# A retention attention and its channel mix on one core: blocks 6 to 11 take K once for turned keys and state products

## The chip, the cores and the metric

The kernel runs on one core of one Trainium2 chip. The metric is the device time of one execution in microseconds (us), and lower is better. Five engines of the core work beside one another: PE multiplies matrices, DVE and ACT work on vectors, POOL (GpSimd) does here one product and otherwise issues DMAs, and SP issues DMAs alone. Each engine takes its own instructions in the order in which the program holds them and waits at one until what it needs is there. PE loads one operand of a product as weights (LDWEIGHTS) and then streams the other past it (MATMUL); such a pair is called a pass here. What PE computes lands in PSUM, which has eight banks of 512 float32 per partition; a bank can be written anew once its readers are done.

## The reference

A retention with a recurrent state and per-head decay, and behind it a channel mix with squared ReLU and a gate:

```python
for t in range(S):                              # B, H, S, D = 4, 8, 768, 64
    state = gamma * state + einsum('bhd,bhe->bhde', k[:, :, t], v[:, :, t])
    y[:, :, t] = scale * einsum('bhd,bhde->bhe', q[:, :, t], state)
x = y.transpose(0, 2, 1, 3).reshape(B, S, H * D)
x_prev = concatenate([zeros, x[:, :-1]], axis=1)
xk = mu_k * x + (1 - mu_k) * x_prev             # xr with mu_r
k = maximum(xk @ w_k, 0)                        # 512 -> 1024
v = k * k @ w_v                                 # 1024 -> 512
out = 1 / (1 + exp(-(xr @ w_r))) * v
```

## The kernel before

The 4 x 768 tokens are cut into twelve blocks of 256, three to a batch: blocks 0, 3, 6 and 9 begin a batch. In a block the retention is done by products instead of one token after another. Per block n:

- `lq`, `lk`, `lv` load Q, K and V (float16 for Q and K, cast by GpSimd's DMAs). `vs` multiplies V by the decay and rounds it (L253).
- `Tq` and `Tk` turn Q and K with PE: a product with an identity (L278; L272 in blocks 0 to 3), `Eq` and `Ek` copy the turned halves from PSUM to SBUF (L241, on ACT). A turn of a block is 32 passes that give 64 columns each.
- `S` multiplies turned keys and queries (L318 in blocks 6 to 11), `M` masks the result and takes it to SBUF (L354, DVE).
- `C` is the state product K x V (L366 in blocks 6 to 11, L384 in 2 to 5): K is the stationary operand, V the moving one; 32 passes of 64 columns, 24 where the batch ends. `U` adds the earlier state (L419, DVE, or an ACT copy at L243), `G` applies the block's decay (L424, ACT).
- `I` and `J` multiply the carried state and Q (L441), `Y` the masked scores and V (L462, L478, L489); they add up in one pair of banks. `D` scales that into x, channels on partitions (L514, DVE).
- `dx` and `X` make the shifted mixes xk and xr (L529, L558, L552, DVE). `K.n.g` are the keys of the channel mix (L572 where two blocks are taken together, L582 else), `Qa` their ReLU out of PSUM (L591, ACT), `Qb` the square (L599, L603, ACT). `R` is the gate product (L612) and `s` its sigmoid (L618, ACT), `V.n.t.h` one half of a value product (L624, four passes of 512 columns), `O` the gated result (L630, DVE), `st` its store on SP's queue.
- `z` are products of zeros that fill PE's time near the start (L703, L710).

The order of all this is written out by hand: a string ORDER of some 750 words, which the kernel's last loop goes through from front to back. A word is a piece of the work, the PSUM banks behind an @ and the engine behind a ~ (v DVE, a ACT, p GpSimd's queue, s SP's queue, none PE). `C.4@67` is the state product of block 4 in banks 6 and 7; `Qa.2.0~a` the ReLU of the first keys of block 2 on ACT. So each engine gets its pieces in the string's order, and a piece waits for the pieces it reads from, for the readers of the bank that it writes, and for a DMA's buffer to come free. What a load waits for is what last read its buffer: Q, K and V have four buffers each, the scaled V three, block n using number n mod 4 or n mod 3.

Masks and identities are built on DVE at the start by comparing a row of counts with a column of numbers (`masks`, L680), `mu8` receives the mix factors, which PE turns and ACT copies (L691, L694).

Of the kernel before, what the change touches and what calls it, by code (L numbers as in the profile page):

```python
# [33 lines left out]
lk.3~p vs.2~v Tq.2@1 X.1.1.2~v K.1.3@6 K.1.0@0 C.2@7 U.2.0~v lv.3~p Eq.2~a S.2.1@23 M.2.1~v S.2.0@45
M.2.0~v Qb.0.3~a lv.4~p K.1.1@1 X.1.1.1~v Qa.1.0~a t.0.1.0~a K.1.2@7 I.2@23 Qb.0.1~a Qa.1.1~a wv.0~p
Qb.0.2~a Tq.4@01 Eq.4~a Y.2 Qa.1.3~a Qb.1.1~a X.0.1.3~v X.1.1.3~v R.1.1@4 Tk.4@01 Ek.4~a J.2 R.1.0@6
Qa.1.2~a s.1.0~a X.0.1.2~v X.0.1.1~v X.0.1.0~v R.0.1@5 s.0.1~a s.1.1~a R.0.0@7 s.0.0~a S.4.1@01
Qb.1.0~a D.2~v dx.2~v X.2.0.2~v X.2.0.0~v S.4.0@23 Tq.3@4 Eq.3~a X.2.0.1~v wv.1~p X.2.0.3~v Tk.3@7
lq.5~p Ek.3~a K.2.2@5 Qa.2.2~a K.2.3@4 M.4.1~v M.4.0~v Qa.2.3~a Qb.2.3~a lk.6~p S.3.1@67 M.3.1~v
S.3.0@01 vs.3~p C.3@23 U.3.0~a Qb.2.2~a K.2.1@4 Qa.2.1~a K.2.0@2 Qa.2.0~a I.3@45 lq.6~p vs.4~v  # L40
C.4@67 U.3.1~v X.2.1.1~v V.0.1.0@3 M.3.0~v V.1.0.0@2 G.3~a U.4.0~v I.4@01 X.2.1.3~v U.4.1~v J.3
Qb.1.3~a Y.4 Qb.2.0~a lk.5~p X.2.1.2~v X.2.1.0~v Y.3 D.3~v dx.3~v V.0.0.0@7 V.0.1.1 O.0.1~v Tq.5@45
J.4 D.4~v dx.4~v R.2.0@6 Qb.2.1~a V.0.0.1 O.0.0~v X.3.0.1~v Eq.5~a Qb.1.2~a V.1.0.1 X.3.0.2~v
O.1.0~v Tq.6@01 Eq.6~a Tk.6@45 Ek.6~a st.0.0~s lk.7~p st.1.0~s V.1.1.0@3 V.1.1.1 O.1.1~v s.2.0~a
R.2.1@0 s.2.1~a lv.5~p X.3.0.0~v X.3.0.3~v Tk.7@67 Ek.7~a G.4~a S.6@45 M.6~v Tk.5@23 Ek.5~a vs.5~v
V.2.0.0@0 K.3.2@1 Qa.3.2~a K.3.0@6 S.5.0@23 M.5.0~v S.5.1@45 C.5@1 U.5.0~v K.3.3@7 Qb.3.2~a Qa.3.0~a
lq.7~p K.3.7@6 Qa.3.3~a Qa.3.7~a lv.6~p lq.8~p vs.6~v M.5.1~v V.2.0.1 st.0.1~s I.5@67 O.2.0~v
st.2.0~s C.6@23 U.6.0~a U.6.1~v U.6.2~v K.3.6@1 Qa.3.6~a lk.9~p X.3.1.3~v Y.5 Tq.7@45 Eq.7~a U.6.3~v
X.3.1.2~v I.6@01 J.5 X.3.1.0~v D.5~v X.3.1.1~v Qb.3.3~a G.6~a V.2.1.0@2 K.3.1@3 V.2.1.1 O.2.1~v
Qb.3.7~a Qa.3.1~a Qb.3.1~a dx.5~v K.3.4@4 K.3.5@5 Qa.3.5~a X.5.0.0~v X.5.0.3~v R.3.1@2 s.3.1~a  # L50
lv.7~p Qa.3.4~a X.5.0.1~v Qb.3.4~a R.3.0@5 R.4.0@2 s.3.0~a s.4.0~a Qb.3.0~a X.5.0.2~v vs.7~v K.5.2@4
S.7@67 st.1.1~s M.7~v Qb.3.5~a Y.6 Qb.3.6~a lv.10~p C.7@23 U.7.0~v X.5.1.1~v Qa.5.2~a K.5.0@5
R.4.1@6 Qa.5.0~a D.6~v s.4.1~a V.4.0.0@4 V.4.0.1 V.3.1.0@5 U.7.1~v Qb.5.0~a X.5.1.3~v U.7.2~v I.7@01
X.5.1.2~v U.7.3~v Tq.8@67 Eq.8~a X.5.1.0~v O.4.0~v lv.8~p vs.8~v Qb.5.2~a lq.10~p lk.8~p Tk.8@23
Ek.8~a V.3.1.1 V.3.0.0@4 C.8@67 O.3.1~v st.2.1~s st.3.1~s Y.7 dx.6~v D.7~v Tq.10@23 V.3.0.1 Eq.10~a
G.7~a dx.7~v X.6.0.2~v V.4.1.0@5 R.5.1@2 s.5.1~a K.5.3@0 Qa.5.3~a R.5.0@2 U.8.0~v O.3.0~v V.4.1.1
lv.9~p lk.10~p lq.9~p Tk.10@01 s.5.0~a U.8.1~v X.6.0.1~v Ek.10~a X.6.0.0~v Tk.9@23 Ek.9~a K.5.1@7
# [27 lines left out]
def kernel(  # L85
# [51 lines left out]

    Q16 = ring("q16_", 4, [H, 2 * D], F16)
    K16 = ring("k16_", 4, [H, 2 * D], F16)
    V32 = ring("v32_", 4, [H, 2 * D], F32)  # L140
    VS = ring("vs_", 3, [2, H, D], F16)
# [17 lines left out]
    mu8 = const.tile([P, P], F32, name="mu8")  # L159
# [17 lines left out]
    count = OS(3)[:, 0:P]  # L177

# [223 lines left out]

    def carried(n, c):
        return TG[c if half(n) else 2 * c](n)

    def summed(e, n, c):
        src = banks("C", n)
        if half(n):
            src = src[:, c % 2, c // 2 * NJ * D : (c // 2 + 1) * NJ * D]
            last = c == 3  # L410
        else:
            src = (src[:, c] if more(n) else src)[:, 0 : NJ * D]
            last = c == 1
        src = src.rearrange("p (j d) -> p j d", j=NJ)
        to = T32(n) if last else carried(n, c + 1)
        if c == 0 and first(n):
            copy(e, to, src)
        else:
            nc.vector.tensor_tensor(out=to, in0=src, in1=carried(n, c), op=ALU.add)  # L419
# [81 lines left out]
    def yout(e, n, u=None):  # L501
# [16 lines left out]
        )  # L518

# [154 lines left out]
    def masks(e, part):  # L674
        for out, col, op in (
            ((ident, 0, ALU.is_equal),),
            ((causal[:, 0], 1, ALU.is_ge), (causal[:, 1], 1, ALU.is_gt)),
            ((step, 2, ALU.is_ge), (below, 0, ALU.is_ge)),
        )[part]:
            e.tensor_scalar(  # L680
                out=out, in0=count[:, 0 : out.shape[-1]], scalar1=mark[:, col : col + 1], scalar2=None, op0=op
            )
# [50 lines left out]
    def load_wk(e, h):  # L733
        f = slice(h * dff // 2, (h + 1) * dff // 2)
        nc.gpsimd.dma_start(out=wk16[:, :, f], in_=wks[:, :, f])
# [4 lines left out]
    def load_wv(e, h):  # L740
# [59 lines left out]
```

## Time and profile before

| what | value |
|---|---|
| median of 3 runs | 153.06 us |
| lowest and highest | 152.80 and 153.37 us |
| the profiled execution: time, span | 152.84 us, 151.1 us |
| granted PE clock over the span | 1.000 |
| PE, DVE, ACT, POOL busy | 143.7, 127.7, 103.4, 55.3 us |
| value products (L624) | 184 passes, 44.1 us |
| gate, keys together, keys (L612, L572, L582) | 23.4, 23.0, 23.2 us |
| turns of Q and K in 64 columns (L278) | 256 and 256 passes, 3.6 and 3.4 us |
| state products of blocks 6 to 11 (L366) | 176 passes, 2.7 us |

The span runs from the first to the last instruction of the profiled execution; 1.74 us of its time lie around it. Busy times are unions: passes overlap in the pipeline, so that a pass has a mean of, say, 195 ns and 256 of them 3.6 us all the same. In a timeline a row is a run of like instructions with its start, its length, its engine, its line, the operation with its tiles, the stationary operand's size for PE (64*64), the shape and the count; [0.65 <-DVE tg L419] is idle time ahead of it and what ended it. The length of a run of passes has the pipeline's last end in it, so what a run costs is read from its start to the start of the next.

### The profile page before, as it was taken

To read this page: it belongs to the slowest core of one execution; us is meant where nothing else is said; L and a number is where in the kernel's file an instruction comes from. 1 tells how busy PE (TensorE), PEld (TensorE's weight loads), DVE (VectorE), ACT (ScalarE), POOL (GpSimd) and SP (SyncE) were. 2 spreads that over 40 slices of the span, in tenths; PEclk is the share of its full clock that TensorE was granted. 3 is DMA by queue.
4 is the path that set the end of the run, shared out by engine and by line. 5 is a ranking of instruction groups with operands and counts; after the bars stand their busy time and mean duration, and the time that the engine had idled before them with its cause. 6 is when DMAs were issued, how large, how long until landed. Compare 5 with 4: busy or idle time off the path is not lost.

```text
span 151.1 us, 5533 instructions
## 1 busy us (share of the span) xinstructions
PE 143.7 (95%) x2426; PEld 82.6 (55%) x2426; DVE 127.7 (85%) x211; ACT 103.4 (68%) x195; POOL 55.3 (37%) x65
## 2 busy tenths in 40 slices
PE   7968799999999999999999999999999999999991
PEld 3345487748754554547465564548456444655450
DVE  7976999999999999999999999999799999400432
ACT  3475979799944895879567786999604756839420
POOL 7954988478867209996700000000000000000000
PEclk9999999999999999999999999999999999999999
DMA  4999999999999999999999019311000005500433
GB/s 135 229 235 192 204 233 195 169 250 213 196 166 206 232 267 101 265 299 196 229 172 126 4 40 282 105 38 42 0 4 0 4 0 205 212 0 0 152 130 139
DMA packets 45624, 22.16 MB, mean 147 GB/s; under 512 B 37400, under 2 KB 41248, under 8 KB 45600
## 3 DMA queue, kind: packets, MB, share of 16 engines
q0 software_dynamic: 38704, 14.42, 74.7%
q1 hardware_dynamic: 6592, 7.21, 14.3%
q8 instruction: 19, 0.31, 0.8%
q10 hardware_dynamic: 304, 0.18, 0.4%
q14 instruction: 5, 0.04, 0.1%
HBM read 24.16 MB, written 6.29 MB: 202 GB/s over the span
## 4 chain that ended last, share of the span: by engine, by line
PE 73%; DMA 12%; POOL 11%; issue 2%; DVE 0%; POOLq 0%
PE ps L624 27%; PE ps L572 14%; PE ps L612 12%; PE ps L582 8%; DMA q<-in_q_dram 7%; DMA v<-in_v_dram 5%; PE ps L278 3%; POOL q L235 3%; POOL k L230 2%; PE ps L441 2%; POOL vs L253 2%; PE ps L366 1%; PE ps L462 1%; POOL v L230 1%; PE ps L642 1%
## 5 line engine op out<-in xcount | busy, mean ns | idle before, releaser
L624 PE MATMUL ps<-wv,k2s 128*128 128x512 f16 x184 | 44.1, 380 | 0.0
L591 ACT ACTIVATE kr<-ps 128x512 f32<-128x512 f32 x48 | 27.8, 594 | 12.4 <-PE ps L582 6.4
L624 PEld LDWEIGHTS <-k2s 128*128 128x128 f16 x184 | 17.1, 98 | 18.9 <-ACT k2s L603 0.4
L630 DVE SCALAR_TENSOR_TENSOR os<-ps,rs 128x512 f32<-128x512 f32 x23 | 15.7, 684 | 11.8 <-ACT rs L618 9.5
L612 PE MATMUL ps<-wr,xr 128*128 128x512 f16 x96 | 23.4, 379 | 0.0
L582 PE MATMUL ps<-xk,wk 128*128 128x256 f16 x192 | 23.2, 273 | 0.0
L572 PE MATMUL ps<-xk,wk 128*128 128x512 f16 x96 | 23.0, 379 | 0.0
L618 ACT ACTIVATE rs<-ps 128x512 f32<-128x512 f32 x24 | 13.6, 597 | 12.5 <-PE ps L612 12.4
L230 POOL DMA_DIRECT2D k<-in_k_dram x20 | 17.7, 902 | 11.5 <-PE ps L384 6.9
L582 PEld LDWEIGHTS <-wk 128*128 128x128 f16 x192 | 18.0, 98 | 3.8
L241 ACT COPY qT<-ps 128x1024 f16<-128x1024 f16 (+1 forms) x13 | 12.3, 946 | 9.4 <-PE ps L278 7.8
L558 DVE SCALAR_TENSOR_TENSOR xr<-dx,mu,xT 128x256 f16<-128x256 f32 (+1 forms) x32 | 17.9, 577 | 0.1
L230 POOL DMA_DIRECT2D v<-in_v_dram x18 | 16.1, 912 | 3.5 <-DMA wr<-in_moe_w_r_dram 1.9
L558 DVE SCALAR_TENSOR_TENSOR xk<-dx,mu,xT 128x256 f16<-128x256 f32 (+1 forms) x32 | 17.0, 580 | 0.2
L354 DVE TENSOR_TENSOR a<-ps,c_sb 128x1024 f16<-128x1024 f32 (+1 forms) x14 | 14.5, 1065 | 0.9 <-PE ps L339 0.6
L603 ACT ACTIVATE k2s<-kr 128x512 f16<-128x512 f32 x24 | 14.8, 631 | 0.3
L572 PEld LDWEIGHTS <-wk 128*128 128x128 f16 x96 | 9.1, 98 | 10.6
L612 PEld LDWEIGHTS <-xr 128*128 128x128 f16 x96 | 9.1, 98 | 10.6 <-DVE xr L558 0.3
L599 ACT ACTIVATE k2s<-kr 128x512 f16<-128x512 f32 x24 | 14.5, 626 | 0.3
L241 ACT COPY kT<-ps 128x1024 f16<-128x1024 f16 (+1 forms) x13 | 12.2, 944 | 2.8 <-PE ps L272 1.9
L529 DVE TENSOR_TENSOR dx<-xT 128x1024 f32<-128x1024 f32 x11 | 13.4, 1221 | 0.2
L253 DVE TENSOR_TENSOR vs<-v,csm_sb 128x1024 f16<-128x1024 f32 x10 | 12.2, 1217 | 0.2
(73 smaller groups left out, 165.9 us busy)
## 6 DMA issues: line engine op xcount, KB each, us to landing
out_dram<-os SPq DMA_DIRECT2D x23, 256.0 KB, 2.4
v<-in_v_dram POOLq DMA_DIRECT2D x18, 256.0 KB, 7.6
q<-in_q_dram POOLq DMA_DIRECT2D x11, 256.0 KB, 8.3
k<-in_k_dram POOLq DMA_DIRECT2D x21, 128.0 KB, 8.7
v<-in_v_dram POOLq DMA_DIRECT2D x2, 512.0 KB, 6.9
wk<-in_moe_w_k_dram POOLq DMA_DIRECT2D x2, 512.0 KB, 10.7
wv<-in_moe_w_v_dram POOLq DMA_DIRECT2D x2, 512.0 KB, 9.6
wr<-in_moe_w_r_dram POOLq DMA_DIRECT2D x1, 512.0 KB, 9.5
```

Source lines behind the costliest of these rows:

```text
L230: e.dma_start(out=dst[:, :, i * D : i * D + D], in_=src[:, i * P : i * P + P].rearrange("h p d -> p h d"),)
L241: e.copy(out=out, in_=in_)
L253: e.tensor_tensor(out=VS(n), in0=V32(n).rearrange("p h (i d) -> p i h d", i=2), in1=gks[:, int(half(n) or wide(n)), :, :, None].to_broadca ...
L354: nc.vector.tensor_tensor(out=a_full(n)[:, i, :, j0:j1], in0=pairs(banks("S", n, i, j0))[:, :, j0:j1], in1=(below if wide(n) else causal[: ...
L558: nc.vector.scalar_tensor_tensor(out=XM[w](k)[:, j, t0:t1], in0=DX(k)[:, j, t0:t1], scalar=mu[:, w * NCO + j : w * NCO + j + 1], in1=x[:, ...
L572: nc.tensor.matmul(banks("K", n, g), lhsT=wk16[:, co, g * P : g * P + P], rhs=XM[0](k)[:, co, :], start=(co == 0), stop=(co == NCO - 1),)
L582: nc.tensor.matmul(pz[:, i, :], lhsT=wk16[:, co, fo * P : fo * P + P], rhs=XM[0](k)[:, co, m * TM + t0 : m * TM + t1], start=(i == 0 and c ...
L591: nc.scalar.activation(out=kr, in_=banks("K", n, g, *u), func=AF.Relu)
L603: nc.scalar.activation(out=K2(n)[:, w * g : w * g + w, t0:t1], in_=kr.rearrange("p a t -> p (a t)").rearrange("p (i t) -> p i t", i=w), fu ...
L612: nc.tensor.matmul(banks("R", n, tb), lhsT=XM[1](k)[:, co, t : t + P], rhs=wr16[:, co, :], start=(co == 0), stop=(co == NCO - 1),)
L624: nc.tensor.matmul(banks("V", n, tb), lhsT=K2(n)[:, fo, tb * P : tb * P + P], rhs=wv16[:, fo, :], start=(fo == 0), stop=(fo == NFO - 1),)
L630: nc.vector.scalar_tensor_tensor(out=OS(2 * n + tb), in0=banks("V", n, tb), scalar=1.0 / (KSC * KSC), in1=RS(2 * n + tb), op0=ALU.mult, op ...
```

## The change

**One pass of K for two products (blocks 6 to 11).** `Tk`, `Ek` and `C` go; `TC.n.i` and `Ec.n.i` come, i the half of the block. K is the stationary operand, as in `C`, and the moving one is 128 columns wide: 64 of an identity and 64 of V. So a pass gives the turned K and the state product side by side. Each of the three buffers of scaled V has got 64 columns more in front, which hold an identity (`VI`, place 0), and the moving operand is taken with a step from the identity to the head's V.

```diff
+    def VS(n):
+        return VI(n)[:, 1:].rearrange("p (i h) d -> p i h d", i=2)
-    VS = ring("vs_", 3, [2, H, D], F16)
+    VI = ring("vs_", 3, [2 * H + 1, D], F16)
...
+    def both(n, i):
+        return banks("TC", n, i).rearrange("p u (j x t) -> p u j x t", j=NJ, x=2)
+
+    def turned_state(e, n, i):
+        ps = both(n, i)
+        for j in range(NJ):
+            for u in range(2):
+                for a, h, jo, hp in heads(j):
+                    k = 1 + i * H + h
+                    x = slice(0, 2) if more(n) or not (u and i) else slice(0, 1)
+                    nc.tensor.matmul(
+                        ps[low(a), u, j, x], lhsT=K16(n)[low(u), h, i * D : i * D + D],
+                        rhs=VI(n)[low(u), 0 : k + 1 : k][:, x],
+                        start=(j == 0), stop=(j == NJ - 1), skip_group_check=True,
+                    )
+
+    def turned_k_part(e, n, i):
+        copy(
+            e, KT(n)[:, :, i].rearrange("c j (u p) -> c u j p", u=2), both(n, i)[:, :, :, 0],
+        )
```

Both results lie in a pair of banks per half, four banks to a block; the turned keys are float32 there. `Ec` copies them to SBUF as float16, one copy for each half. `U` reads the states out of the same banks, with a step:

```diff
+        if merged(n):
+            src = both(n, c // 2)[:, c % 2, :, 1]
```

The identities of the three buffers are built in `cm.2` behind the two masks there:

```diff
-            ((step, 2, ALU.is_ge), (below, 0, ALU.is_ge)),
+            ((step, 2, ALU.is_ge), (below, 0, ALU.is_ge))
+            + tuple((VI(i)[:, 0], 2, ALU.is_equal) for i in range(3) if MERGED),
```

**A fence.** `w.n` on ACT reads a few elements of the bank pair of I into a small tile, between `I.n` and `Y.n`:

```diff
+    def fence(e, n):
+        us = slice(0 if half(n) or not first(n) else 1, 2)
+        e.copy(out=fenced[:, us], in_=pairs(banks("I", n))[:, us, :, 0:C:W])
```

`mu8` shares a tile with a result buffer, and `wk` is loaded by words that name quarters; the two transfers are the old ones.

**Order.** The zero products are other ones: before, three long ones ahead of the first turn, then a short one and five pairs of short ones; now two long and two short ones ahead of the first turn, then one long and twelve short ones in groups of 1 to 3. The pair directly ahead of Tq.1 is gone. Apart from these the first 196 pieces stand in the order that they had, but the PSUM banks are dealt anew for all of them; behind piece 196 (from the words behind `lk.5~p` on) order and banks are new. One stretch of the first 196:

```diff
-S.3.0@01 vs.3~p C.3@23 U.3.0~a Qb.2.2~a K.2.1@4 Qa.2.1~a K.2.0@2 Qa.2.0~a I.3@45 lq.6~p vs.4~v
-C.4@67 U.3.1~v X.2.1.1~v V.0.1.0@3 M.3.0~v V.1.0.0@2 G.3~a U.4.0~v I.4@01 X.2.1.3~v U.4.1~v J.3
+S.3.1@23 M.3.1~v S.3.0@45 vs.3~p C.3@67 U.3.0~a Qb.2.2~a K.2.1@0 Qa.2.1~a K.2.0@1 Qa.2.0~a I.3@23
+lq.6~p vs.4~v C.4@01 U.3.1~v X.2.1.1~v V.0.1.0@6 M.3.0~v V.1.0.0@7 G.3~a U.4.0~v I.4@45 X.2.1.3~v
```

Where it speaks of block 3 behind that point: the keys of blocks 3 and 4 now stand in the order 2, 4, 7, 3, 6, then C.5, S.6 and S.5, then 1, 0, 5, K.3.6 and K.3.1 both in bank 0. `C.5` (block 5) stands ahead of S.6, and Y.5 between I.6 and Y.6.

The first place that the order shows is PE from the last keys of block 1 to Tk.4, before. q_0 and k_0 hold block 4's Q and K, qT_79 is block 2's turned Q, tg_2_95 the state that it multiplies (I.2), vs_76 block 2's V and a_2_85 its masked scores (Y.2); L612 are the gate products R.1.1.

```order
L582 MATMUL ps<-xk_102,wk_133 128x256
L441 MATMUL ps<-qT_79,tg_2_95 64x128 [waits DVE_49]
...
L278 LDWEIGHTS q_0_62 [waits DMASW5_49]
L278 MATMUL ps<-c_sb,q_0_62 64x64 [waits Activation_49]
...
L478 MATMUL ps<-a_2_85,vs_76 64x128 [waits DVE_49]
...
L612 LDWEIGHTS xr_105 [waits DVE_49]
...
L278 LDWEIGHTS k_0_66 [waits DMASW7_49]
L278 MATMUL ps<-c_sb,k_0_66 64x64 [waits Activation_49]
```

The same stretch of PE now:

```order
L618 MATMUL ps<-xk_102,wk_133 128x256
...
L473 MATMUL ps<-qT_79,tg_2_95 64x128 [waits DVE_49]
...
L287 LDWEIGHTS q_0_62 [waits DMASW5_49]
L287 MATMUL ps<-c_sb,q_0_62 64x64 [waits DVE_49]
...
L510 MATMUL ps<-a_2_85,vs_76 64x128
...
L648 LDWEIGHTS xr_105 [waits DVE_49]
...
L287 LDWEIGHTS k_0_66 [waits DMASW7_49]
L287 MATMUL ps<-c_sb,k_0_66 64x64 [waits Activation_49]
...
L287 MATMUL ps<-c_sb,k_0_66 64x64 [waits Activation_49]
```

The wait for DVE stands at Tq.4 instead of Y.2, since Tq.4 now writes banks 4 and 5, those of S.2.0; and Tk.4 waits for ACT at two of its passes, once for each of its banks 2 and 3.

The second place is PE from the keys K.2.0 (L582, wk_133) over I.3 (tg_0_93) to the state product C.4 (k_0_66 and vs_75 are block 4's K and V), before:

```order
L582 MATMUL ps<-xk_103,wk_133 128x256 [waits Activation_49]
...
L441 MATMUL ps<-qT_77,tg_0_93 64x128
...
L384 LDWEIGHTS k_0_66
L384 MATMUL ps<-vs_75,k_0_66 64x64 [waits DVE_49]
```

And now:

```order
L618 MATMUL ps<-xk_103,wk_133 128x256 [waits Activation_49]
...
L473 LDWEIGHTS tg_0_93 [waits Activation_49]
L473 MATMUL ps<-qT_77,tg_0_93 64x128 [waits DVE_49]
...
L393 LDWEIGHTS k_0_66 [waits DVE_49]
L393 MATMUL ps<-vs_75,k_0_66 64x64 [waits Activation_49]
...
L393 MATMUL ps<-vs_75,k_0_66 64x64 [waits Activation_49]
```

C.4 has got two waits for ACT, at its first and its third pass, one for each of the banks 0 and 1 that K.2.1 and K.2.0 wrote; I.3 has got one for DVE.

The third place is the end of GpSimd's queue: the last loads of K, V and Q. v_3 is the buffer of block 11's V; k_2, k_0, k_3 and k_1 are those of K of blocks 10, 8, 11 and 9. Before, lv.11 stood in SP's queue, behind ten stores, and on GpSimd's queue:

```order
L230 DMA v_0_70<-in_v_dram 128x8x64
...
L230 DMA k_0_66<-in_k_dram 128x8x64 [waits DMASW1_49]
...
L230 DMA v_1_71<-in_v_dram 128x8x64 [waits DMASW3_49]
...
L230 DMA k_2_68<-in_k_dram 128x8x64 [waits DMASW5_49,PE_49]
...
L235 DMA q_3_65<-in_q_dram 128x8x128 [waits DMASW0_49,PE_49]
L230 DMA k_3_69<-in_k_dram 128x8x64 [waits DMASW1_49,PE_49]
```

And now, from lk.10 to lq.11:

```order
L239 DMA k_2_68<-in_k_dram 128x8x64 [waits DMASW7_49,PE_49]
...
L239 DMA v_3_73<-in_v_dram 128x8x64 [waits DMASW1_49,DVE_49]
...
L239 DMA k_0_66<-in_k_dram 128x8x64 [waits DMASW3_49]
...
L239 DMA k_3_69<-in_k_dram 128x8x64 [waits DMASW5_49,PE_49]
...
L239 DMA v_1_71<-in_v_dram 128x8x64 [waits DMASW2_49]
...
L244 DMA q_3_65<-in_q_dram 128x8x128 [waits DMASW4_49,PE_49]
```

lv.11 stands between lk.10 and lk.8 and waits for DVE, which reads the buffer's last content (block 7's V); lk.8, lk.11, lq.9, lk.9, lv.9 and lq.11 come behind it in the same queue.

135 lines of the change are left out of this document (70 added, 65 removed).

## The prediction

> **What bounds the kernel now.** I read the page first, then the busy time by windows, then the timelines of single engines. The page, parts 1, 2 and 4:
>
> ```profile
> span 151.1 us, 5533 instructions
> PE 143.7 (95%) x2426; PEld 82.6 (55%) x2426; DVE 127.7 (85%) x211; ACT 103.4 (68%) x195; POOL 55.3 (37%) x65
> PE   7968799999999999999999999999999999999991
> DVE  7976999999999999999999999999799999400432
> PE 73%; DMA 12%; POOL 11%; issue 2%; DVE 0%; POOLq 0%
> ```
>
> PE is busy in nearly every slice, and 73% of the chain that ended last is PE. The windows say where (span, then PE, PEld, DVE, ACT, POOL):
>
> ```profile
> 0.00:20.00 20.00, 16.02 (x319) 9.03 (x320) 16.49 (x43) 11.95 (x25) 15.40 (x21) 1.00 1.31 200
> 20.00:37.70 17.70, 17.49 (x293) 12.78 (x291) 17.36 (x27) 16.38 (x30) 13.50 (x16) 1.00 1.51 212
> 30.40:147.90 117.50, 117.43 (x1949) 65.70 (x1948) 100.61 (x153) 82.37 (x154) 32.50 (x37) 1.00 0.78 133
> ```
>
> From 30.4 to 147.9 PE works 117.43 of 117.50 us: it waits for nobody. So from 30.4 on every us of PE work that the change removes is gained, and every new PE wait is lost in full; there is no idle time to swallow it. Ahead of 30.4 PE and DVE (17.36 of 17.70) wait for one another.
>
> **Part by part: the merged products.** For blocks 6 to 11 the 32 passes that turn K and the 32 (24 in blocks 8 and 11) of the state product become 32 passes of K against identity and V, 128 columns wide (64 columns in 8 of those in 8 and 11). The rows, starts first:
>
> ```profile
> 49.38 1.90 PE L624 MATMUL ps<-wv,k2s 128*128 128x512 f16 x8
> 51.12 1.03 PE L612 MATMUL ps<-wr,xr 128*128 128x512 f16 x4
> 52.08 0.45 PE L278 MATMUL ps<-c_sb,k 64*64 64x64 f16 x32
> 52.35 0.44 PE L318 MATMUL ps<-qT,kT 64*64 64x64 f16 x32
> 89.19 0.45 PE L366 MATMUL ps<-vs,k 64*64 64x64 f16 x32
> 89.47 0.46 PE L462 MATMUL ps<-a,vs 64*64 64x64 f16 x32
> 13.12 0.64 PE L489 MATMUL ps<-a,vs 64*64 64x128 f16 x32
> 13.59 0.28 PE L441 MATMUL ps<-qT,tg 64*64 64x128 f16 x4
> 16.84 0.31 PE L441 MATMUL ps<-qT,tg 64*64 64x128 f16 x8 [0.65 <-DVE tg L419]
> 16.98 0.39 PE L339 MATMUL ps<-qT,kT 64*64 64x128 f16 x16
> ```
>
> From start to start, 32 passes of 64 columns take 0.27 (turned K) and 0.28 (state), together 0.55; 32 of 128 columns take 0.47 (L489). That is 0.08 less in each of four blocks; in 8 and 11 0.48 gives way to about 0.42. I take -0.5 for all six. The ends: the eight L441 passes of 128 columns took 0.14, or 17 ns each, by which 32 cost 0.54 and nothing is saved; at best -0.7.
>
> The Trainium skill's page "TensorE: Matmul & The Clock Gate", section "Back-to-back issue gap", speaks against this: a pass of 1 to 64 columns takes about 60 cycles and one of 128 takes 134, so that two narrow passes are cheaper than one wide one; shared by four tiles that is an estimate of +0.05 in each block and +0.3 for the six. The trace does not agree: 0.55 against 0.47 for the same count.
>
> Between big products and small ones PE loses about 0.1: four gate passes took 0.96 ahead of a turn (51.12 to 52.08), where eight passes in a row take 1.74 (49.38 to 51.12, 0.87 for four). The new order has as many stretches of small work as the old one, but inside them it puts block 5, with its own tile shapes, between pieces of block 6 twice (C.5 ahead of S.6, and Y.5 between I.6 and Y.6): two shape changes more, +0.2 (0 to 0.3).
>
> **Place A: Tq.4 in the banks of S.2.0.** The first 196 pieces keep their order, but their PSUM banks are dealt anew, and PE waits for banks. In the rows of the section on the change the wait for DVE (M.2.0, which reads banks 4 and 5) has moved from Y.2 up to Tq.4, and Tk.4 has a second wait for ACT. The timelines of PE, DVE and ACT there:
>
> ```profile
> 28.37 0.31 PE L441 MATMUL ps<-qT,tg 64*64 64x128 f16 x8
> 28.51 0.42 PE L278 MATMUL ps<-c_sb,q 64*64 64x64 f16 x32
> 28.88 0.64 PE L478 MATMUL ps<-a,vs 128*64 128x128 f16 x16
> 30.42 0.45 PE L278 MATMUL ps<-c_sb,k 64*64 64x64 f16 x32
> 26.48 2.35 DVE L354 TENSOR_TENSOR a<-ps,c_sb 128x1024 f16<-128x1024 f32 x2
> 29.00 1.01 ACT L241 COPY qT<-ps 128x1024 f16<-128x1024 f16 x1 [0.21 <-PE ps L278]
> 29.91 0.60 ACT L591 ACTIVATE kr<-ps 128x512 f32<-128x512 f32 x1
> ```
>
> M.2.0 ends at 28.83. Tq.4 now starts at 28.88 instead of 28.51; its copy, 0.49 behind it, at 29.37; Qa.1.3 is next in ACT's queue and ends at 30.88 instead of 30.51. Tk.4 now stands in banks 2 and 3, the latter that of K.1.3, so it waits for Qa.1.3: 30.93 instead of 30.42. That is +0.5 (at least 0.2, by which Tq.4 pushes Y.2 and the gate products; at most 0.6).
>
> **Place B: C.4 in the bank of K.2.0.** Before, C.4 used banks 6 and 7; now 0 and 1, and K.2.0 has just written 1: in the rows of the section on the change its first and third pass wait for ACT. The timelines:
>
> ```profile
> 39.93 0.30 PE L441 MATMUL ps<-qT,tg 64*64 64x128 f16 x4
> 40.16 0.44 PE L384 MATMUL ps<-vs,k 128*64 128x64 f16 x16
> 39.22 0.60 ACT L591 ACTIVATE kr<-ps 128x512 f32<-128x512 f32 x1
> 40.09 0.60 ACT L591 ACTIVATE kr<-ps 128x512 f32<-128x512 f32 x1 [0.28 <-PE ps L582]
> ```
>
> K.2.0 ends where I.3 starts, at 39.93; its eviction Qa.2.0 runs from 40.09 to 40.69. Only I.3 (0.23) lies between, so the third pass of C.4 waits until 40.74 where C.4 started at 40.16: +0.55 (0.5 to 0.6). ACT was idle ahead of Qa.2.0, so a PE that comes later only moves both. What is late next is U.4.0 behind C.4, and two value products (eight passes like those that took 1.74) cover that.
>
> **Behind piece 196.** Groups by line and form:
>
> ```profile
> L241 ACT COPY kT<-ps 128x1024 f16<-128x1024 f16 x11 | 11.0, 1010 | 0.9 <-PE ps L278 0.9
> L241 ACT COPY kT<-ps 128x512 f16<-128x512 f16 x2 | 1.2, 586 | 1.9 <-PE ps L272 1.9
> L599 ACT ACTIVATE k2s<-kr 128x512 f16<-128x512 f32 x24 | 14.5, 626 | 0.3
> L694 ACT COPY mu<-ps 128x8 f32<-128x8 f32 x1 | 0.2, 183 | 0.0
> ```
>
> ACT gets two copies of 586 ns for one of 1010, and a fence of about 183 ns (16 elements; the nearest row has 8) in each of six blocks: 6 x 0.35 = 2.1 us on an engine busy 68%, free except where PE waits for ACT soon after. K.3.1 takes bank 0 from K.3.6 with only C.5, S.6 and both S.5 between: about 1.0 us of PE. ACT has Qa.3.7, Qa.3.4, Qa.3.3 and Qb.3.3 to finish first (some 0.5 each in a row, from 1.5 before K.3.6 ends), so Qa.3.6 is done 1.2 behind it: +0.2 (0 to 0.4). The fence of block 6 stands behind two Qa/Qb pairs, and Y.6, then TC.7.0 behind Qa.3.5, wait for it; near the end V.9.1.0 takes bank 7 from K.11.1. I allow +0.15 for these (0 to 0.4). U reads PSUM with a step now; I cost that at nothing, and the same 64-element runs speak for it.
>
> **The ramp.** DVE builds three identities more in cm.2, ahead of everything it does:
>
> ```profile
> 3.10 1.61 DVE L680 TENSOR_SCALAR c_sb<-os,csm_sb 128x128 f16<-128x128 f32 x5
> 4.18 0.55 DVE L718 COPY gy_sb<-csm_sb 128x4 f32<-128x4 f32 x1
> 7.40 1.22 DVE L253 TENSOR_TENSOR vs<-v,csm_sb 128x1024 f16<-128x1024 f32 x1
> 11.58 0.59 PE L710 MATMUL ps<-zero 128*128 128x512 f16 x2 [0.80 <-DVE a L354]
> 12.10 0.64 PE L272 MATMUL ps<-c_sb,q 128*64 128x128 f16 x16
> 13.91 1.23 DVE L514 TENSOR_TENSOR xT<-ps,gy_sb 128x1024 f32<-128x1024 f32 x1 [1.19 <-PE ps L441]
> ```
>
> The five masks of before start within 1.08 (3.10 to 4.18), 0.2 each; three narrow ones put vs.0 some 0.5 later and C.0 with all behind it some 0.35. Against that, the zero products between the first mask of the scores and Tq.1 (11.58 to 12.10) are gone. D.0 at 13.91, behind which DVE is busy nearly without a break (the third row of the page's slices), stays within a tenth or two by this: 0 (-0.4 to +0.6).
>
> **The sum.** -0.5 + 0.2 + 0.5 + 0.55 + 0.2 + 0.15 + 0 = +1.1 us. The profiled execution took 152.84, 0.22 below the median of 153.06; so 152.84 + 1.1 = 153.9, and as a median 154.2. All lower ends together give -0.4, all upper ones +2.9; not all fall on one side, so this case's own range is 153.5 to 155.0.
>
> **Rivals.** 0.5%, about what a measurement can tell from no change, is 0.8 us.
>
> *Not slower: the banks come free in time.* If at A, B and behind K.3.6 PE finds its banks free, as it does everywhere after 30.4 now, only -0.5 + 0.2 and 0.2 of small waits are left: 153.0 with the 153.06 of the median. For it speaks that PE does not wait once in 117.5 us now; against it, that at B nothing but 0.23 of PE work covers an eviction of 0.60. It decides where the waits come to less than 1.1 in all. 0.26.
>
> *Faster: the ramp is what changes.* The dropped zeros (0.5) reach D.0, DVE's unbroken run moves up 0.4, and at A and B the waits are covered too: 153.06 - 0.5 + 0.2 - 0.4 = 152.4. For it speaks that ahead of 30.4 PE loses 4 us of the first 20 (16.02 busy), so that there is something to win; against it, the three masks and the rows on A and B. 0.13.
>
> *The merged product saves nothing.* At L441's 17 ns a pass (0.54 for 32) the first term is 0: 154.7. By the page's cycles it would be 155.0. The 32-pass row speaks against it. 0.10.
>
> *GpSimd's queue blocks.* lv.11 now stands in that queue. It waits for vs.7 on DVE (the row of v_3_73 in the section on the change), and lk.8, lk.11, lq.9, lk.9, lv.9 and lq.11 stand behind it.
>
> ```profile
> k<-in_k_dram POOLq DMA_DIRECT2D x21, 128.0 KB, 8.7
> ```
>
> By PE's order vs.7 falls near 62, so lk.8 lands by about 73, and TC.8.1 is due near 79. If vs.7 were later than 68, PE would stall; at 2 us, 156. 0.05.
>
> **How the numbers follow.** The forecast has 0.46, and 0.85 of it lies over the 0.8 us; with the last two rivals (0.15) that makes 0.54 for slower. The first rival and the forecast's lower edge make 0.33 for the same, the second rival 0.13 for faster. The range must hold 8 in 10: from 152.3 to 155.4 it takes in the first three rivals and the forecast with its own 153.5 to 155.0, and leaves out the fourth rival and the ends at which several costs fall on one side, about 0.15 together. Without the second rival it would hold less than 8 in 10.
>
> **What would show it.** In the profile after: PE waits of about 0.5 for ACT at C.4 and Tk.4 near 41 and 31, of 0.2 behind K.3.6; L422 with 32 passes in 0.47; D.0 at 13.8 to 14.1. It is wrong if PE between 30 and the end is as unbroken as before, or if D.0 comes over half a us off.

## The result, and the profile after

| | kernel before | changed kernel |
|---|---|---|
| first comparison, the runs that count | 153.05 us median (152.80 to 153.37) | 154.83 and 154.49 us |
| ratio of these, 95% interval | | 1.0096 [1.0068, 1.0124] |
| second comparison (label e0_again) | 153.05 us median (152.54 to 153.90) | 154.50, 154.55, 156.05, 156.43, 156.48 us |
| ratio, 95% interval | | 1.0167 [1.0116, 1.0218] |
| profiled execution: time, span | 152.84, 151.1 us | 154.83, 153.1 us |

Not counted in the comparisons here and below are the changed kernel's two runs of 157.35 and one of 157.39 us (granted clock 0.989) and, of later kernels, 156.95 and 157.57 (label e9_forced, 0.989 and 0.988), three from 172.74 to 174.85 (e5_before_twice, 0.960 to 0.961) and one of 155.81 (e11_tail_bank, 0.999). At full clock the changed kernel has two times, about 154.6 and about 156.3; the kernel before has one. The forecast was 154.2. The profile of the run of 154.83 comes first: the page's part 1.

```profile
PE 144.7 (95%) x2253; PEld 82.7 (54%) x2253; DVE 128.2 (84%) x214; ACT 104.9 (69%) x207; POOL 57.1 (37%) x67
```

The stretch from 30.4 to 147.9 us, asked of the kernel after (span, then PE, PEld, DVE, ACT, POOL, granted clock, DMA share, GB/s):

```profile
30.40:147.90 117.50, 116.95 (x1768) 64.67 (x1765) 99.87 (x152) 84.73 (x167) 34.76 (x39) 1.00 0.77 129
```

From 30.4 to 147.9 PE now has 0.55 us without work, where it had 0.07; and it started that stretch late. PE and ACT at place A and place B, and the last product:

```profile
28.98 0.31 PE L473 MATMUL ps<-qT,tg 64*64 64x128 f16 x8
29.49 0.45 PE L287 MATMUL ps<-c_sb,q 64*64 64x64 f16 x32 [0.20 <-DVE a L363]
31.40 0.59 PE L287 MATMUL ps<-c_sb,k 64*64 64x64 f16 x32
31.81 0.30 PE L473 MATMUL ps<-qT,tg 64*64 64x128 f16 x8
41.00 0.30 PE L473 MATMUL ps<-qT,tg 64*64 64x128 f16 x4
41.17 0.60 ACT L627 ACTIVATE kr<-ps 128x512 f32<-128x512 f32 x1 [0.28 <-PE ps L618]
41.82 0.41 PE L393 MATMUL ps<-vs,k 128*64 128x64 f16 x14 [0.37 <-ACT kr L627]
42.16 0.60 PE L660 MATMUL ps<-wv,k2s 128*128 128x512 f16 x2
148.79 1.04 PE L678 MATMUL ps<-wv,k2s 128*128 128x256 f16 x8
```

The last product of the kernel before:

```profile
146.85 1.04 PE L642 MATMUL ps<-wv,k2s 128*128 128x256 f16 x8
```

Read against the rows of before, piece by piece: I.2 starts at 28.98 instead of 28.37, so 0.61 came from the ramp. From I.2 to Tq.4 it takes 0.51 instead of 0.14, and Tk.4 takes 0.41 (0.27 without its waits, below): 0.51 at place A. I.3 is 1.07 late, V.0.1.0 behind C.4 1.63 (42.16 against 40.53): 0.56 at place B, where 14 of the 16 passes stand behind the eviction that began at 41.17. The last product is 1.94 late: 0.31 came from everything behind piece 196. The ramp on DVE:

```profile
4.21 1.39 DVE L717 TENSOR_SCALAR vs<-os,csm_sb 128x64 f16<-128x64 f32 x3
5.03 0.58 DVE L755 COPY gy_sb<-csm_sb 128x4 f32<-128x4 f32 x1
8.14 1.22 DVE L262 TENSOR_TENSOR vs<-v,csm_sb 128x1024 f16<-128x1024 f32 x1
14.27 1.23 DVE L546 TENSOR_TENSOR xT<-ps,gy_sb 128x1024 f32<-128x1024 f32 x1 [0.92 <-PE ps L473]
25.05 1.23 DVE L262 TENSOR_TENSOR vs<-v,csm_sb 128x1024 f16<-128x1024 f32 x1 [0.27 <-DMA v<-in_v_dram]
```

The three identities take DVE from 4.21 to 5.03, 0.82. vs.0 starts 0.74 later than before, D.0 0.36. The last row is a transfer that was late in this run: about 0.3 of the 0.61. In the six other traces with the identities in cm.2 and no such wait there, I.2 starts at 28.64 to 28.70, so that the ramp itself is 0.3.

### The profile page after: what moved, and what is told of

Read it like the earlier page. It is cut to its first block, busy times and chain, and to the rows that moved or that the text cites. A ratio compares the mean times of both kernels' runs of the same rounds, so it can differ in the third digit from the quotient of the medians.

```text
span 153.1 us, 5210 instructions
## 1 busy us (share of the span) xinstructions
PE 144.7 (95%) x2253; PEld 82.7 (54%) x2253; DVE 128.2 (84%) x214; ACT 104.9 (69%) x207; POOL 57.1 (37%) x67
## 4 chain that ended last, share of the span: by engine, by line
PE 69%; DMA 10%; ACT 8%; POOL 5%; DVE 3%; issue 3%; DVEq 0%; ACTq 0%; POOLq 0%
PE ps L660 26%; PE ps L648 12%; PE ps L608 11%; DMA v<-in_v_dram 10%; PE ps L618 7%; ACT kr L627 4%; ACT k2s L635 2%; PE ps L422 2%; PE ps L287 2%; POOL q L244 2%; PE ps L473 2%; DVE a L363 1%; PE ps L327 1%; PE ps L494 1%; PE ps L678 1%
## 5 line engine op out<-in xcount | busy, mean ns | idle before, releaser
L660 PE MATMUL ps<-wv,k2s 128*128 128x512 f16 x184 | 44.8, 380 | 0.1
L627 ACT ACTIVATE kr<-ps 128x512 f32<-128x512 f32 x48 | 27.2, 596 | 11.8 <-PE ps L608 9.6
L608 PE MATMUL ps<-xk,wk 128*128 128x512 f16 x96 | 22.3, 379 | 0.0
L239 POOL DMA_DIRECT2D v<-in_v_dram x20 | 17.8, 895 | 8.3 <-DVE vs L262 2.0
L363 DVE TENSOR_TENSOR a<-ps,c_sb 128x1024 f16<-128x1024 f32 (+1 forms) x14 | 14.5, 1064 | 0.7 <-PE ps L348 0.5
L244 POOL DMA_DIRECT2D q<-in_q_dram x12 | 10.8, 904 | 0.9 <-PE ps L660 0.5
```

Of the source, the lines that this page charges most:

```text
L239: e.dma_start(out=dst[:, :, i * D : i * D + D], in_=src[:, i * P : i * P + P].rearrange("h p d -> p h d"),)
L363: nc.vector.tensor_tensor(out=a_full(n)[:, i, :, j0:j1], in0=pairs(banks("S", n, i, j0))[:, :, j0:j1], in1=(below if wide(n) else causal[: ...
L608: nc.tensor.matmul(banks("K", n, g), lhsT=wk16[:, co, g * P : g * P + P], rhs=XM[0](k)[:, co, :], start=(co == 0), stop=(co == NCO - 1),)
L627: nc.scalar.activation(out=kr, in_=banks("K", n, g, *u), func=AF.Relu)
L660: nc.tensor.matmul(banks("V", n, tb), lhsT=K2(n)[:, fo, tb * P : tb * P + P], rhs=wv16[:, fo, :], start=(fo == 0), stop=(fo == NFO - 1),)
```

## Experiments

**The waits for banks, and the two times.** My theory was the sum: the waits at A and B, a little from the new order, a saving from the merge, nothing from the ramp. Its first rival was that the waits cost nothing, because something else stands right behind them. The changed kernel was run again as a base:

> The changed kernel once more, as the base for the runs beside it. Every theory expects the ratio of the result, 1.0096 over the kernel before (1.007 to 1.012).

Measured: 1.0167 [1.0116, 1.0218], outside of what was expected, with times at 154.5 and at 156.0 to 156.5. Its profile fell on a run of 156.48, and shows where the 2 us are (DVE, POOL, PE):

```profile
34.34 3.74 DVE L594 SCALAR_TENSOR_TENSOR xk<-dx,mu,xT 128x256 f16<-128x256 f32 x4
35.08 1.91 POOL L262 TENSOR_TENSOR vs<-v,csm_sb 128x1024 f16<-128x1024 f32 x1
37.33 2.37 PE L618 MATMUL ps<-xk,wk 128*128 128x256 f16 x16 [1.31 <-DVE xk L594]
```

The same place in the run of 154.83:

```profile
34.68 1.67 DVE L594 SCALAR_TENSOR_TENSOR xk<-dx,mu,xT 128x256 f16<-128x256 f32 x4
36.28 1.22 DVE L363 TENSOR_TENSOR a<-ps,c_sb 128x1024 f16<-128x1024 f32 x1
36.28 1.91 POOL L262 TENSOR_TENSOR vs<-v,csm_sb 128x1024 f16<-128x1024 f32 x1
```

Four mixes X.2.0 take 1.67 when GpSimd's product vs.3 starts at their end, and 3.74 when it starts among them: one of the four took 2.54 instead of 0.48, by the view of that line in the run of 156.48 (shortest, median and longest in ns):

```profile
L594 DVE SCALAR_TENSOR_TENSOR xk<-dx,mu,xT x4: 473/480/2543, 34.3 to 37.6; 128x256 f16<-128x256 f32 x4
```

K.2.2 on PE waits for them. That made a second theory, the collision, which no part of my prediction had. The mask M.4.1 (L363), beside the same product in the second fence, takes its usual 1.22.

The old banks in the first 196 pieces (one line of many; behind them the banks are renamed alike):

```diff
-lq.6~p vs.4~v C.4@01 U.3.1~v X.2.1.1~v V.0.1.0@6 M.3.0~v V.1.0.0@7 G.3~a U.4.0~v I.4@45 X.2.1.3~v
+lq.6~p vs.4~v C.4@67 U.3.1~v X.2.1.1~v V.0.1.0@3 M.3.0~v V.1.0.0@2 G.3~a U.4.0~v I.4@01 X.2.1.3~v
```

> The changed kernel with the PSUM banks of the kernel before for the first 196 pieces, and the same dealing as now behind them with the banks renamed. Bank theory: the waits at Tq.4 and Tk.4 (0.52 together in the trace) and at C.4 (0.55) are gone and nothing takes their place: 1.05 us less than the changed kernel, a ratio of about 1.003 over the kernel before. Rival, another limit stands right behind (DVE, which is busy 9.6 of 10 us from 20 to 30): at most half of it comes back, 1.006 or more.

Measured: 153.47 us (153.40 to 153.68, 12 runs), ratio 1.0032 [1.0016, 1.0047]. PE at A and B:

```profile
28.70 0.31 PE L473 MATMUL ps<-qT,tg 64*64 64x128 f16 x8
28.84 0.42 PE L287 MATMUL ps<-c_sb,q 64*64 64x64 f16 x32
30.76 0.44 PE L287 MATMUL ps<-c_sb,k 64*64 64x64 f16 x32
31.03 0.28 PE L473 MATMUL ps<-qT,tg 64*64 64x128 f16 x8
40.54 0.44 PE L393 MATMUL ps<-vs,k 128*64 128x64 f16 x16
40.91 1.25 PE L660 MATMUL ps<-wv,k2s 128*128 128x512 f16 x5
```

Tq.4 stands 0.14 behind I.2 again, Tk.4 takes 0.27, C.4 runs through in 0.37. Against the changed kernel's 154.5 to 154.8 that is 1.0 to 1.4 less, where 1.05 was expected: the bank theory holds. And no run of the twelve is at 156: with the waits went the second time.

To test the collision, first the load lq.6 was put ahead of vs.3 in GpSimd's queue:

```diff
-S.3.1@23 M.3.1~v S.3.0@45 vs.3~p C.3@67 ...
+S.3.1@23 M.3.1~v S.3.0@45 lq.6~p vs.3~p C.3@67 ...
```

> The changed kernel with the load lq.6 ahead of GpSimd's product vs.3 instead of behind it, so that the product starts 0.9 us later. Collision theory: the times of 156 us and more come from runs in which that product starts while DVE makes the mixes X.2.0, one of which then takes 2.54 us instead of 0.48; now it starts behind them always, no run is above 155.4, and the median is 154.5 to 155.1 (C.3 waits 0.4 for vs.3 where the product was late already). Rival, the slow runs have another cause (the clock, DMA): half of the runs are at 156 and more as before.

Measured: 154.77, 154.92, 155.01, 155.73, 155.73, 156.94; ratio 1.0156 [1.0118, 1.0194]. Expected was none above 155.4, so this did not settle it. In the profiled run of 155.73 the mixes take their 1.67, and the product that PE needs for C.3 came too late instead: PE waits 1.1 us there. The run of 156.94, at full clock, has no trace; what it lost is not known.

Then a wait that does nothing else, a product of two elements per partition on GpSimd that reads the last mix:

```diff
+    def wait_pool(e):
+        e.tensor_tensor(out=poolf, in0=XM[0](place[2][0])[:, 3, 0:2], in1=gd[:, 0:2], op=ALU.mult)
...
-S.3.1@23 M.3.1~v S.3.0@45 vs.3~p C.3@67 ...
+S.3.1@23 M.3.1~v S.3.0@45 wp~p vs.3~p C.3@67 ...
```

> The changed kernel with a product of two elements per partition on GpSimd ahead of vs.3, which reads what the last of the four mixes X.2.0 wrote: so vs.3 can't start before the mixes are done. Nothing else is moved. Collision theory: no run at 156 and more any more, all between 154.3 and 155.2, median about 154.7. Rival, the runs at 156 have another cause: they stay, about half of all runs. GpSimd gets about 0.2 us, and C.3 may wait 0.2 for it.

Measured: 154.50, 154.52, 154.62, 154.75, 154.77; ratio 1.0090 [1.0070, 1.0111]. DVE and POOL:

```profile
34.36 1.68 DVE L595 SCALAR_TENSOR_TENSOR xk<-dx,mu,xT 128x256 f16<-128x256 f32 x4
36.12 0.19 POOL L602 TENSOR_TENSOR poolf<-xk,csm_sb 128x2 f16<-128x2 f16 x1 [0.17 <-DVE xk L595]
36.28 1.90 POOL L263 TENSOR_TENSOR vs<-v,csm_sb 128x1024 f16<-128x1024 f32 x1
```

The second time is gone, in five runs, with nothing moved but the start of vs.3 (0.17 of waiting): the collision theory holds so far. The other way round, the kernel before was driven into it by a second dx.2:

```diff
-... Qb.1.0~a D.2~v dx.2~v X.2.0.2~v ...
+... Qb.1.0~a D.2~v dx.2~v dx.2~v X.2.0.2~v ...
```

> The kernel before with the subtraction dx.2 on DVE done twice in a row (the same result), so that DVE comes to the mixes X.2.0 1.25 us later (34.9 to 36.6 instead of 33.6 to 35.3) and GpSimd's product vs.3, which starts at 35.74, starts among them. Collision theory: one mix takes some 2.4 us instead of 0.48, the keys K.2.2 behind it come 3 us later, and the time is 155.5 to 156.2, ratio 1.016 to 1.02, in all runs. Rival, the two don't disturb each other: 1.2 us of DVE at most, 154.3 or less, ratio 1.008 or less.

Measured: 154.12, 155.68, 156.16, 156.18; ratio 1.0149 [1.0102, 1.0196]. The run of 156.16:

```profile
35.38 3.32 DVE L558 SCALAR_TENSOR_TENSOR xk<-dx,mu,xT 128x256 f16<-128x256 f32 x4
36.39 2.03 POOL L253 TENSOR_TENSOR vs<-v,csm_sb 128x1024 f16<-128x1024 f32 x1
```

Three of four fell into the expected 155.5 to 156.2; the fourth is at the 154.3 that the extra subtraction costs alone. "In all runs" was too much, since GpSimd's start depends on transfers. With this and the run before, the collision is shown as the cause of the second time.

**The ramp.** The identities as a part of their own (cm.3), directly ahead of D.0:

```diff
-            ((step, 2, ALU.is_ge), (below, 0, ALU.is_ge))
-            + tuple((VI(i)[:, 0], 2, ALU.is_equal) for i in range(3) if MERGED),
+            ((step, 2, ALU.is_ge), (below, 0, ALU.is_ge)),
+            tuple((VI(i)[:, 0], 2, ALU.is_equal) for i in range(3) if MERGED),
...
-... Y.0 D.0~v ...
+... Y.0 cm.3~v D.0~v ...
```

> The changed kernel with the three identities built later on DVE, directly ahead of D.0, where DVE waits 0.92 us for PE. Mask theory: vs.0 starts at 7.4 instead of 8.14, C.0 and what hangs on it by about 0.6 earlier, the first keys (K.0.0) by 0.46: 0.5 to 0.6 us less than the changed kernel, a ratio of about 1.006. Rival, the zero products: the long pair ahead of C.1 still holds C.1, U.1.0 and I.1 back, so that K.0.0 gains 0.2 at most and the ratio stays at 1.008 or above.

Measured: 154.17 us (153.91 to 154.44), ratio 1.0074 [1.0048, 1.0100]; against the 154.50 and 154.55 of the changed kernel without the collision in the same comparison, 0.35 less. DVE, and PE at I.2:

```profile
7.45 1.22 DVE L262 TENSOR_TENSOR vs<-v,csm_sb 128x1024 f16<-128x1024 f32 x1
12.96 0.57 DVE L717 TENSOR_SCALAR vs<-os,csm_sb 128x64 f16<-128x64 f32 x3
13.97 1.23 DVE L546 TENSOR_TENSOR xT<-ps,gy_sb 128x1024 f32<-128x1024 f32 x1 [0.43 <-PE ps L473]
28.36 0.31 PE L473 MATMUL ps<-qT,tg 64*64 64x128 f16 x8
```

vs.0 is back at 7.45, and D.0 at 13.97 instead of 14.27: 0.3 earlier, not 0.6, and the ratio lies between the mask theory's 1.006 and the zeros theory's 1.008. But I.2 starts at 28.36, as in the kernel before (28.37): of the 0.3 that the ramp costs without a late transfer, the identities are all that a trace can tell. All three parts undone together (old banks, late identities, old zeros; the lines of before are those of the kernel with the old banks):

```diff
-... z.1@2 z.1@3 Tq.0.0.2@0 Tk.0.0.2@1 gy.1~v mt@2 Ek.0.0.2~a Eq.0.0.2~a z.3@4 ...
+... Tq.0.0.2@0 Tk.0.0.2@1 gy.1~v z.1@2 mt@2 Ek.0.0.2~a Eq.0.0.2~a ...
...
-... Y.0 D.0~v ...
+... Y.0 cm.3~v D.0~v ...
```

> Old banks for the first 196 pieces, identities built ahead of D.0 and the zero products of the kernel before together; merge, fence, GpSimd's queue and the new order behind piece 196 stay. Sum theory: the ramp costs 0.6 at the end of it, of which the masks are 0.3 and a zero product ahead of the second turn of K 0.3; with both gone PE runs as before up to piece 196, and what is left is the order behind with its waits and the merge: 152.9 to 153.1, ratio 0.999 to 1.000. Rival, masks and zeros take each other's place with something else: 153.4, ratio 1.003.

Measured: 153.21 us (153.11 to 154.25), ratio 1.0020 [1.0005, 1.0036], between the two expectations. Whether the zeros matter was asked again at the end, by the new zeros with all else as in the kernel of the next part (label e11_tail_bank):

```diff
-t.0.0.3~a t.0.0.2~a t.0.0.1~a lv.2~p z.2@6 S.1.1@23 M.1.1~v C.1@01 U.1.0~v z.2@7 I.1@23
+t.0.0.3~a t.0.0.2~a t.0.0.1~a lv.2~p z.2@6 S.1.1@23 M.1.1~v z.4@7 C.1@01 U.1.0~v z.1@4 I.1@23
```

> The kernel with old banks, late identities and the other bank for V.9.1.0, with the zero products of the changed kernel instead of the old ones. If the new zeros are the better ones once the identities are out of the way (152.9 to 153.2 with the old ones; late identities alone gave 0.45 with the new ones): 153.47 - 0.45 - 0.28 = 152.75, ratio about 0.998 over the kernel before, and faster than both kernels. Rival, the long zero product ahead of C.1 and the one ahead of the second turn of K cost 0.2 to 0.3: 153.2 to 153.4, ratio 1.001 to 1.003.

Measured: 153.28 us (152.85 to 153.84), ratio 1.0016 [1.0000, 1.0032]; with the old ones 1.0008 [0.9989, 1.0028]. The intervals overlap: the zeros cost nothing that can be measured, and the 152.75 was a miss. A part of the spread comes from GpSimd: in the profiled runs of 153.66 (combined kernel) and 153.73 (this one) C.3 waits 0.37 and 0.57 for vs.3, in that of 152.96 (label e11_tail_bank) not at all.

**The tail.** In the changed kernel PE and ACT at V.9.1.0, which takes the bank of K.11.1:

```profile
138.15 1.03 PE L648 MATMUL ps<-wr,xr 128*128 128x512 f16 x4
138.64 0.60 ACT L627 ACTIVATE kr<-ps 128x512 f32<-128x512 f32 x1
139.29 1.02 PE L660 MATMUL ps<-wv,k2s 128*128 128x512 f16 x4
```

Four gate passes take 0.86 elsewhere, here 1.14 to the next product, which starts 0.05 behind the ReLU's end. One number, in the combined kernel:

```diff
-s.11.0~a V.9.1.0@3 ...
+s.11.0~a V.9.1.0@1 ...
```

> The kernel with old banks, old zeros and late identities (153.21 us) with one number changed: V.9.1.0 takes another bank than that of K.11.1, whose ReLU it waits for (0.28 in the trace of the changed kernel). If PE is what the end waits for there, 0.25 to 0.3 less: about 152.9, ratio 0.998 to 1.0005. Rival, ACT's queue in the last 15 us (sigmoids and squares one behind another) is what ends last: no change, 153.2, ratio 1.001 to 1.002.

Measured: ratio 1.0008 [0.9989, 1.0028], median 153.25 (152.84 to 153.71 in eleven of twelve runs, one of 155.81 is not counted, and has no trace; combined kernel 1.0020). PE there, at V.0.1.0 and at the last product:

```profile
40.52 1.90 PE L660 MATMUL ps<-wv,k2s 128*128 128x512 f16 x8
136.50 1.03 PE L648 MATMUL ps<-wr,xr 128*128 128x512 f16 x4
137.37 1.03 PE L660 MATMUL ps<-wv,k2s 128*128 128x512 f16 x4
146.87 1.04 PE L678 MATMUL ps<-wv,k2s 128*128 128x256 f16 x8
```

0.87 from start to start: the wait is gone in the trace, and the whole stretch is shorter by it. From V.0.1.0 to the last product PE takes 106.35 here, 106.63 in the changed kernel (42.16 to 148.79) and 106.32 before (40.53 to 146.85). The times by themselves can't tell 0.28 from the spread.

**The merge.** Undone in place, it should have shown its saving:

```diff
-TC.6.1@23 TC.6.0@67 U.6.0~a V.1.1.1 K.3.2@1 Ec.6.1~a O.1.1~v Ec.6.0~a U.6.1~v ...
+C.6@23 Tk.6@67 U.6.0~a V.1.1.1 K.3.2@1 O.1.1~v Ek.6~a U.6.1~v ...
```

> The changed kernel with the merge alone undone: for blocks 6 to 11 one piece C and one piece Tk in the places and banks of the two merged pieces, one copy Ek for the two Ec; identities, fence, order and all else as in the changed kernel. Merge saves 0.5 (the term of my sum): 0.4 to 0.5 us more than the changed kernel, ratio 1.012 to 1.013. Rival, it saves nothing: within 0.15 us of the changed kernel, 1.009 to 1.011. Second rival, the two copies of 0.59 cost more than the passes save: less than the changed kernel, 1.008 or below.

Measured: 158.55 us, ratio 1.0353 [1.0319, 1.0387], far outside all three. The order is made for two halves with two copies; with one piece of each kind PE gets waits of 0.5 to 1.05 us that the changed kernel does not have, for instance in C.7:

```profile
67.62 0.32 PE L374 MATMUL ps<-vs,k 64*64 64x64 f16 x17
68.99 0.32 PE L374 MATMUL ps<-vs,k 64*64 64x64 f16 x15 [1.05 <-issue]
```

So this says nothing on the price of a pass. The next two ask for that price alone, by doing both kinds twice: the turn and the state product in the kernel before, the merged product in the kernel with the old banks.

```diff
-            for j in range(j0, j1):
+            for j in [*range(j0, j1)] * (2 if a and half(n) else 1):
...
-        for j in range(NJ):
+        for j in [*range(NJ)] * 2:
```

> The kernel before, with the turn of K and the state product of blocks 6 to 11 each done twice in a row (192 and 176 passes of 64 columns more, the same result). By the rows of the trace (0.27 and 0.28 for 32 passes) PE gets 3.1 us more, all of it on the path: about 156.2 us, a ratio of 1.020. It is the price of what the merge takes away.

> The kernel with the changed order and the old banks for the first 196 pieces (153.47 us, ratio 1.0032), with the merged product of K done twice in a row (192 passes more, 184 of 128 columns and 8 of 64, the same result). Price of what the merge brings: by 0.47 for 32 passes 2.7 us more, 156.2 us, ratio 1.021, so that the merge saves 0.4; if it saves nothing, at 17 ns a pass, 3.1 to 3.2 us more, ratio 1.024; if a wide pass costs more than two narrow ones, 3.5 us or more, ratio 1.026 or above.

Measured: 172.07 us, ratio 1.1263 [1.1232, 1.1293], and 156.97 us, ratio 1.0247 [1.0221, 1.0273]. Neither total is a price: the first kernel ran at a granted clock of 0.960 to 0.980 and waited longer than all its added passes:

```profile
PE ps L278 <- issue: 5.2, 4, 2.2
PE ps L366 <- issue: 5.1, 1, 5.1
```

The second waited 0.78 once. But the traces hold undisturbed runs of passes, at a granted clock of 1.00. Turns and state products twice, 64 passes each with what follows, in the kernel before:

```profile
54.79 0.71 PE L278 MATMUL ps<-c_sb,k 64*64 64x64 f16 x64
55.32 0.45 PE L318 MATMUL ps<-qT,kT 64*64 64x64 f16 x32
102.28 0.71 PE L366 MATMUL ps<-vs,k 64*64 64x64 f16 x64
102.81 0.48 PE L462 MATMUL ps<-a,vs 64*64 64x64 f16 x32
```

TC.7.1 of the changed kernel, once:

```profile
74.34 0.42 PE L422 MATMUL ps<-vs,k 64*64 64x128 f16 x16
74.59 0.42 PE L287 MATMUL ps<-c_sb,q 64*64 64x64 f16 x32
```

And twice:

```profile
74.57 0.64 PE L422 MATMUL ps<-vs,k 64*64 64x128 f16 x32
75.05 0.42 PE L287 MATMUL ps<-c_sb,q 64*64 64x64 f16 x32
```

64 narrow passes take 0.53 where 32 took 0.27 and 0.28, so 0.26 and 0.25 for 32 more, 0.51 for both kinds; 32 wide ones take 0.48 where 16 took 0.25, so 0.23 for 16 more, 0.46 for 32. That is 0.05 a block. At the other places where the same pieces stand on both sides of the run, 32 more turns take 0.28 to 0.29, 32 more state products 0.26 to 0.27, and 32 more wide passes 0.44 to 0.46. So the merge saves 0.05 to 0.12 a block, 0.3 to 0.6 for six.

## Why the prediction was right, and where not

- **PE has no slack behind 30.4.** Right: the waits at A, at B and at V.9.1.0 were lost in full, and came back when they were taken away (1.0 to 1.4 us of the time for A and B, 0.28 in the trace for V.9.1.0).
- **Place A, +0.5.** Right, mechanism and size: 0.51, in the two steps foreseen (Tq.4 behind M.2.0, Tk.4 behind Qa.1.3).
- **Place B, +0.55.** Right: 0.56, with 14 of 16 passes behind Qa.2.0.
- **The merged passes, -0.5.** Right within what the doubled passes can tell, 0.3 to 0.6. The rival "saves nothing" is out, by 0.44 to 0.46 against 0.51 to 0.56 for the same work. The Trainium skill's page "TensorE: Matmul & The Clock Gate", section "Back-to-back issue gap", gives about 60 and 134 cycles at 2.4 GHz for passes of 64 and 128 columns; shared by four tiles that is an estimate of 0.20 and 0.45 for 32 passes. The wide rows agree with it (0.44 to 0.46), the narrow ones do not (0.25 to 0.29).
- **K.3.1, +0.2.** Wrong: it starts without a wait. C.5, S.6 and both S.5 take 1.17 in the trace where I had 1.0, and Qa.3.6 is done 1.1 behind K.3.6 where I had 1.2: two errors of 0.1, and the wait is gone.
- **Fence, Y.6, TC.7.0 and V.9.1.0, +0.15.** Under-sized: V.9.1.0 alone waits 0.28. All behind piece 196, merge and shape changes with it, cost 0.31 where the sum had +0.05; with V.9.1.0 in another bank it is 0.03. So the shape changes, the fence and the rest cost about what the merge saves, and no run says how much is whose. The kernel was not tried without the fence, since I.n and Y.n would then write one bank with nothing to order them.
- **The ramp, 0.** This is the term that was mis-sized. The prediction had the identities at 0.5 of DVE and set the dropped zeros against them; they take 0.82, and the zeros give nothing back. The late identities gained 0.35 in time and about 0.3 at I.2. In the profiled run the ramp was 0.61, 0.3 of it a late transfer, and D.0 came at 14.27, outside the 13.8 to 14.1 that the prediction named as a sign.
- **GpSimd's queue.** The rival (lv.11 ahead of lk.8) did not come: TC.8.1 has no wait. But it was GpSimd that gave the changed kernel its second time, by another way that the prediction did not see: it followed when vs.3 would be ready, not what runs beside it.
- **The sum, +1.1.** The runs without the collision lie at +1.4 to +1.8 (154.5 to 154.8): the forecast's own case held, its 154.2 was 0.3 to 0.6 low, by the ramp (0.3) and by what stands behind piece 196 (0.26 more than the sum had). The rivals "not slower" and "faster" are out (the ratio is 1.0068 at the least). With the collision the time is about 156.3, above the range's 155.4. The two counted runs of the first comparison did not have it and three of five in the second did, so it was in part luck that the result fell inside the range.

**Why the collision came with this change.** This is read from starts in a few traces, and not shown by a run of its own. Before, vs.3 started at 35.74, 0.44 behind the mixes (33.63 to 35.30); in the five traces of merged kernels with the old banks it starts 0.37 to 1.03 behind them. The waits at A and the ramp moved the mixes by 1.05 in one run of the changed kernel and by 0.71 in another, while vs.3 moved in these runs by 0.5 (36.28) and by -0.7 (35.08): a load of wv ahead of it in GpSimd's queue waited 0.36 for a transfer of Q in the first and not in the second. So vs.3 started 0.07 ahead of the mixes' end in one and among them in the other. But a shift as large as that between these two would have reached the mixes of the kernel before too, and none of its 73 runs is above 154.56. So this account is not complete. In 48 runs of the four kernels with the old banks and each merged pass done once there is one near 156, the 155.81 without a trace; whether it is the collision is open. Open, too, is what makes a transfer land early or late from run to run, as are the waits for "issue" of the doubled and the unmerged kernels.

No version beats both kernels: with old banks, old zeros, late identities and the tail mended, ratio 1.0008 [0.9989, 1.0028], faster than the changed kernel and the same as the one before. What the merge saves is about what the order behind piece 196 costs.

## What to carry to other kernels

Where an engine is packed, dealing PSUM banks anew is a change of its own: for each product look at who read its bank last, when that eviction ends, and what PE work lies between. Set-up work on an engine that feeds the first products costs its length, so put it into an idle stretch ahead of its first use. And when an order shifts one engine against another, ask not only who waits for whom but which instructions will run side by side.

## What the runs showed of the hardware

A product on GpSimd and a mix on DVE whose two operands both lie in SBUF did not run side by side: beside vs.3 (1.9 to 2.0 us) one mix took 2.54 in one run and 2.12 in another, instead of 0.48. In the first it had begun 0.34 ahead of vs.3, and still ended 0.29 behind it. A mask, with one operand in PSUM, ran beside the same product in its usual 1.22, and so did D.0 beside vs.1 (1.23). The Trainium skill's page "GPSIMD Engine Reference", section "1. Specifications", has the rule: GpSimd's SBUF interfaces are shared with VectorE, and DVE instructions with two SBUF inputs contend. The traces agree, and the mask and D.0 are the other side of the rule; as the mixes are another operation than these two, no run here tells operand places from operations. The prediction should have weighed it.

In the kernel with 368 of PE's 2426 passes doubled the granted clock was 0.960 to 0.980 in all seven runs. The trace of its run at 0.980 shows where it was low (stretch, length, then PE, PEld, DVE, ACT, POOL, granted clock, DMA share, GB/s):

```profile
75.50:80.70 5.20, 0.11 (x15) 0.03 (x5) 0.51 (x1) 1.04 (x3) 2.86 (x4) 0.69 1.72 222
80.70:84.00 3.30, 3.30 (x20) 1.92 (x20) 2.87 (x7) 0.60 (x1) 1.75 (x2) 0.50 1.76 158
```

The first stretch is PE's one wait of 5.09 us, and the clock falls to 0.50 between 77 and 78, some 2 us into it. It stays there until between 84 and 85, some 4 us after PE has started again. From 0 to 75.5 and from 88 on it is 1.00, the doubled passes included, and a wait of 2.19 us (from 49.7 to 51.9) left it at 1.00. So in this run the long wait lowered the clock, and not the passes; the other six have no trace.
